# Attention scores and value products in quarters of TensorE's array, with blocks of 64 keys of two heads and other first loads

## The chip, the cores and the metric

The kernel runs on one core of a Trainium2 chip. The metric is the device time of one execution in microseconds (us); times of several executions are given by their median. The engines are named as in the profile: PE is TensorE (matmuls; its weight loads are PEld), DVE is VectorE, ACT is ScalarE, POOL is GpSimd, and SP is SyncE, which issues most of the DMAs.

## The reference

Eight batches of eight heads, 576 tokens, head dimension 64. Attention keeps, in each row of scores, only what lies within tau of the row's maximum; the result goes through a gated feed-forward block with a convolution of three taps along the tokens.

```python
scores = scale * np.matmul(q, k.transpose(0, 1, 3, 2))
thresh = np.max(scores, axis=-1, keepdims=True) - tau
scores = np.where(scores >= thresh, scores, -1000000000.0)
scores = scores - np.max(scores, axis=-1, keepdims=True)
attn = np.exp(scores)
attn = attn / (np.sum(attn, axis=-1, keepdims=True) + 1e-09)
attn_out = np.matmul(attn, v)
...
h = np.maximum(x @ w_in, 0.0)            # x: heads side by side, 512; h: 1024
conv_out += conv_w[k] * hp[:, k:k + S, :]  # k = 0, 1, 2
gate = 1.0 / (1.0 + np.exp(-conv_out))
return h * gate @ w_out
```

## The kernel before

**Tiling.** A batch's 576 queries are four tiles of 128 and one of 64. Two chunks split them: tiles 0 and 1 (256 queries) and tiles 2, 3 and 4 (320). For each chunk the kernel goes through four pairs of heads. A unit is one tile of queries of one pair. Everything is fp32; a product in fp32 stands in the trace as two matmul records, and the feed-forward splits its operands into high and low parts and takes three products.

**A unit** (`unit`, L526). For each of the two heads TensorE computes 128 x 576 scores (L549): the head dimension of 64 fills half of the array's rows, so the keys are laid out as two halves of 288 on the lower and upper 64 partitions, and two products run side by side, each on 64 rows and 128 columns of the array. Each half goes to a PSUM bank of its own (tile ps_s). VectorE takes the row's maximum (L558), ScalarE the exponential into em (L565), VectorE the mask with the sum (L568), and mostly GpSimd the normalization (L606). Tile 4 has 64 queries, so its unit takes both heads of a pair at once as 128 rows, in four products of 64 rows and 64 columns.

**Transposition.** em holds 1152 keys (both heads) in nine blocks of 128. Each must be turned so that keys lie on partitions (tile eT). Either TensorE transposes blocks into PSUM (ps_t, L665) in groups of four and ScalarE copies them (L660), or a unit is "crossed": it is split into 16-bit halves (L331, L333), written to memory and read back by transposing DMAs (`cross`, L621). The ninth block, and that of the small unit, hold keys of both heads or half a block, and are collected in a group of their own (`odd`, L694).

**Attend** (`attend`, L708). The product with v: one "mixed" step in quarters of the array for the block that holds keys of both heads (L720), then four steps per pair on 128 rows and 64 columns (L729). From the third chunk on two pairs are attended together (`JOINT = 2`), the first pair's four steps ahead of the second's. The sums stand in two PSUM buffers (pa, of the same two that ps_t uses), and ScalarE and VectorE take them out as high and low part (L736, L739).

**Feed-forward.** `mm1` (L758) and `mm2` (L809) use the whole array, and their pieces are strewn between the units of the next chunk.

**Order.** `Plan` records every operation with its reads, writes, cost and rank (place in the program less a lead from AHEAD) and then plays all engines through, so that each takes the ready operation of lowest rank; the order it finds is the program. SWITCH holds its cost of a change between forms of TensorE's work: "rows" (scores and mixed step), "cols" (the other attend steps), "turn" (transpositions), "full" (feed-forward).

**First loads.** `prep` (L488) loads k, q and v of a pair and scales k by an eighth. For the first pair k comes in two parts on ScalarE's queue, and ScalarE scales them; the first three pieces of the weights are issued on ScalarE's queue too (L380), the rest on SP's.

Of the kernel before, what the change touches and what calls it, by code (L numbers as in the profile page):

```python
# [22 lines left out]
AHEAD = {'mask': 0.543, 'norm': 2.382, 'parts': 0.64, 'gate': 1.279, 'evac': 0.244, 'low': 0.0, 's': 8.8, 's4': 8.664, 't': 3.225, 'a': 3.987, 'prep': 7.193, 'w': 2.513, 'load': 10.996}  # L23

LATENCY = {'pe': 159.52, 'act': 151.014, 'dve': 109.122, 'pool': 87.954, 'ring': 1611.881}

HOLD = {'pool': 133.132, 'dve': 108.982}

NORM = (('pool',), ('pool', 'pool', 'pool', 'act'))
# [5 lines left out]
MOE = (2, 3)  # L35
BACKLOG = {'pool': 6860.0, 'dve': 120.0, 'act': 9000000000.0}
WRATE = (1.767, 1.972)
ALT = 2.85
# [4 lines left out]
EARLY = 1  # L43
# [7 lines left out]
JOINT = 2  # L51

FAR = 3
VB = 4
EMS = 5
KEEPK = 1
# [5 lines left out]
CROSS = ((1, 1, 1, 1), (2, 1, 2, 1))  # L62
LATE = {'load': 663.0, 'copy': 114.0, 'rows': -19.0, 'turn': 737.0}

KEEP = {'rows': 3.449, 'cols': 2.129, 'turn': 2.26, 'full': 1.604}
# [187 lines left out]
def tile_tau_attention_gated_ffn(  # L253
    ctx: ExitStack,
    tc: tile.TileContext,
    qd: bass.AP,
    kp: bass.AP,
# [16 lines left out]
    NBLK = 2 * S // P  # L274
    TILES = [(t * P, min(P, S - t * P)) for t in range((S + P - 1) // P)]

# [32 lines left out]
    op("act", 450, lambda: nc.scalar.dma_start(tau_sb[:], tau.broadcast_to([P, 1])), w=[(tau_sb, 0)], ahead=205.0, late=2500)  # L309
# [3 lines left out]
    for x in fews:  # L313
        op("pool", 100, lambda x=x: nc.gpsimd.memset(x[:], LEAST * S), w=[(x, 0)], ahead=200.0)
        op(
            "dve", 150, lambda x=x: nc.vector.tensor_scalar(x[:, 1:4:2], x[:, 1:4:2], 0.0, tau_sb[:], op0=ALU.mult, op1=ALU.add),
            w=[(x, 0)], r=[(tau_sb, 0)], ahead=100.0
        )
# [7 lines left out]

    engines = {"dve": nc.vector, "pool": nc.gpsimd, "act": nc.scalar}
# [31 lines left out]
    def split(src, n, name, high, low, hr, lr, queue="sp"):  # L359
# [19 lines left out]
        def load():  # L379
            (nc.sync if queue == "sp" else nc.scalar).dma_start(flat().bitcast(I64), src)  # L380
# [17 lines left out]
        if queue == "sp":  # L398
            put(2 * n, load, issue=330, w=[hi, lo], ahead=w + AHEAD["load"])
        else:  # L400
            put(2 * n, load, issue=330, queue="act", w=[hi, lo], ahead=90)
# [66 lines left out]
    def load_weight(i):  # L468
        if i < W1N:
            src, dst, c, f = w_in, w1, i % NCB, i // NCB  # L470
        else:
# [4 lines left out]
            src[c * P:(c + 1) * P, f], WN, f"stage_{i}", h, l, *((x, (c, f.start)) for x in dst), "act" if i < 3 else "sp"  # L476
# [11 lines left out]
    def prep(i):  # L488
# [5 lines left out]
        k = whole[i - NP][0] if o and KEEPK else plan.buf(wk, "xk", XKB, [P, S + D], F32, f"k_{i}")  # L494
        q = plan.buf(wk, "q", QB, [P, 2, w], F32, f"q_{i}")
        a = AHEAD["prep"]

        if i:
            if not (o and KEEPK):
                put(S + D, lambda: nc.sync.dma_start(k[:], kp[b, p]), w=[(k, 0), (k, 1)], ahead=a + 2)  # L500
            put(w, lambda: nc.sync.dma_start(q[:], qd[b, p, :, :, o:o + w]), rows=2 * P, w=[(q, 0), (q, 1)], ahead=a + 2)
        else:
            for j, on in enumerate((slice(0, CH), slice(CH, S + D))):
                n = on.stop - on.start
                put(n, lambda on=on: nc.scalar.dma_start(k[:, on], kp[b, p, :, on]), queue="act", w=[(k, j)], ahead=210 - 10 * j)
                put(w, lambda j=j: nc.sync.dma_start(q[:, j], qd[b, p, :, j, o:o + w]), w=[(q, j)], ahead=210 - 10 * j)
        if not (o and KEEPK):
            cuts = [(S + D, lambda: k[:], [(k, 0), (k, 1)])] if i else [
                (on.stop - on.start, lambda on=on: k[:, on], [(k, j)]) for j, on in enumerate((slice(0, CH), slice(CH, S + D)))
# [440 lines left out]
```

## Time and profile before

| what | value |
|---|---|
| median of three runs | 882.54 us (882.46 to 882.92) |
| the profiled execution | 883.45 us, its span 881.7 us |
| granted TensorE clock, mean | 0.998 |
| instructions | 17007 |
| data moved by DMA | 141.53 MB, mean 161 GB/s |

The span runs from the first to the last instruction; what lies around it is 1.75 us here. A row of the groups by shape gives line, engine, operation, out<-in, partitions x elements and count, then busy us, mean ns of one, and the idle time of the engine before these with what ended it. For matmuls, "64*128" is the part of the array, rows by columns. A row of the stretches gives the stretch, its length, then the busy time of PE, PEld, DVE, ACT and POOL with counts, the granted clock, and the DMA share and GB/s. A timeline row gives start, length, engine, line and count of equal instructions merged.

### The profile page before, as it was taken

The page shows a single profiled execution, that of the slowest core. Times are in us where ns is not written, and L with a number is a line of the kernel's source. Part 1 is how long each engine was busy: PE and PEld are TensorE (multiplying, and loading weights), DVE is VectorE, ACT ScalarE, POOL GpSimd, SP SyncE. Part 2 cuts the span into 40 slices and gives each one's busy share as a digit, 9 for nine tenths or more (in the row PEclk, how much of TensorE's full clock was granted, in tenths as well). Part 3 has the DMA queues.
Part 4 walks back from the last instruction along what each step waited for, and adds up shares of the span by engine and source line. Part 5 has one row for each costly group of instructions (what it writes and reads, how often), then busy time and mean ns, then how long its engine had stood idle before and what let it go on. Part 6 is the DMA issues. An engine that isn't in the chain of part 4 may idle for free.

```text
span 881.7 us, 17007 instructions
## 1 busy us (share of the span) xinstructions
PE 851.9 (97%) x5678; PEld 617.5 (70%) x5678; DVE 724.6 (82%) x1905; ACT 670.9 (76%) x1327; POOL 422.2 (48%) x558
## 2 busy tenths in 40 slices
PE   2989999999999999999999999999999999999998
PEld 1445667767678677777778676776777777777796
DVE  3798999988979698987979789996979879996642
ACT  4889888888777687886868777886877868776642
POOL 1465645553546444563536434463544635564321
PEclk9999999999999999999999999999999999999999
DMA  7356136678766765858566675669566475556200
GB/s 257 110 158 191 57 99 169 170 224 213 163 162 161 187 188 148 193 155 235 158 162 139 199 202 161 164 166 237 161 173 146 141 210 158 151 165 159 67 25 37
DMA packets 211063, 141.53 MB, mean 161 GB/s; under 512 B 170144, under 2 KB 186784, under 8 KB 210976
## 3 DMA queue, kind: packets, MB, share of 16 engines
q1 hardware_dynamic: 210112, 138.54, 58.1%
q10 hardware_dynamic: 864, 1.90, 0.6%
q8 instruction: 46, 0.75, 0.3%
q14 instruction: 41, 0.34, 0.1%
HBM read 48.39 MB, written 50.72 MB: 112 GB/s over the span
## 4 chain that ended last, share of the span: by engine, by line
PE 91%; ACT 3%; DVE 3%; DMA 1%; issue 1%; SPq 0%; POOL 0%; ACTq 0%; DVEq 0%; POOLq 0%
PE ph L758 23%; PE po L809 23%; PE ps_s L549 19%; PE pa L729 14%; PE ps_t L665 9%; PE pa L720 2%; DVE few L558 1%; ACT em L565 1%; PE pw_stage L412 1%; DMA q<-in_qd_dram 1%; DVE em L568 1%; ACT eT L660 1%; DMA v<-in_vc_dram 0%; DVE stage_f L393 0%; ACT stage L387 0%
## 5 line engine op out<-in xcount | busy, mean ns | idle before, releaser
L606 POOL TENSOR_SCALAR em<-em,few 128x576 f32<-128x576 f32 x228 | 184.2, 815 | 185.4 <-DVE few L592 168.5
L558 DVE TENSOR_REDUCE few<-ps_s 128x1 f32<-128x576 f32 x288 | 209.3, 748 | 63.3 <-PE ps_s L549 62.7
L565 ACT ACTIVATE em<-ps_s,few 128x576 f32<-128x576 f32 x288 | 208.7, 740 | 56.4 <-DVE few L558 54.7
L568 DVE SCALAR_TENSOR_TENSOR em<-ps_s,few,em 128x576 f32<-128x576 f32 x288 | 226.9, 812 | 23.1 <-ACT em L565 14.2
L758 PE MATMUL ph<-x,w1h 128*128 128x322 f32 (+1 forms) x1024 | 231.8, 305 | 0.6 <-ACT hp L767 0.6
L338 POOL TENSOR_TENSOR gl<-t,gh 128x255 fp32r<-128x255 f32 (+9 forms) x192 | 122.0, 645 | 197.2 <-ACT gh L788 193.7
L549 PE MATMUL ps_s<-k,q 64*128 64x288 f32 (+1 forms) x1280 | 192.0, 439 | 17.6 <-ACT k L331 11.3
L758 PEld LDWEIGHTS ph<-x,w1h 128*128 128x128 f32 x1024 | 171.8, 190 | 16.1 <-issue 12.8
L549 PEld LDWEIGHTS ps_s<-k,q 64*128 64x128 f32 (+1 forms) x1280 | 94.1, 177 | 85.2 <-issue 44.4
L758 PE MATMUL ph<-x,w1l 128*128 128x322 f32 (+1 forms) x512 | 151.0, 295 | 0.0
L729 PE MATMUL pa<-eT,v 128*64 128x320 f32 (+1 forms) x1024 | 132.1, 409 | 0.0
L660 ACT ACTIVATE eT<-ps_t 64x64 f32<-64x64 f32 (+3 forms) x262 | 114.4, 452 | 16.3 <-PE ps_t L665 14.9
L809 PE MATMUL po<-w2h,gh 128*128 128x512 f32 x288 | 117.9, 410 | 0.0
L809 PE MATMUL po<-w2l,gh 128*128 128x512 f32 x288 | 112.7, 391 | 0.0
L809 PE MATMUL po<-w2h,gl 128*128 128x512 f32 x288 | 112.5, 391 | 0.0
L665 PE MATMUL ps_t<-ident,em 128*128 128x128 f32 x682 | 104.4, 281 | 7.6 <-ACT eT L660 3.5
L729 PEld LDWEIGHTS pa<-eT,v 128*64 128x64 f32 x1024 | 70.4, 137 | 58.8 <-issue 15.3
L665 PEld LDWEIGHTS ps_t<-ident,em 128*128 128x128 f32 x682 | 77.0, 141 | 45.6 <-issue 22.0
L758 PEld LDWEIGHTS ph<-x,w1l 128*128 128x128 f32 x512 | 96.5, 189 | 0.2
L331 ACT ACTIVATE parts<-em 128x1152 uint16<-128x1152 uint16 x70 | 81.4, 1163 | 19.0 <-POOL em L606 18.6
L773 DVE SCALAR_TENSOR_TENSOR t<-hp,cr 128x321 f32<-128x321 f32 (+1 forms) x128 | 81.7, 638 | 15.7 <-ACT hp L767 14.7
L333 POOL COPY parts<-em 128x1152 uint16<-128x1152 uint16 x70 | 82.7, 1182 | 15.1 <-DMA rows<-parts 6.9
(68 smaller groups left out, 924.1 us busy)
## 6 DMA issues: line engine op xcount, KB each, us to landing
rows<-parts SPq DMA_DIRECT2D x70, 576.0 KB, 3.1
v<-in_vc_dram SPq DMA_DIRECT2D x36, 288.0 KB, 4.3
q<-in_qd_dram SPq DMA_DIRECT2D x32, 320.0 KB, 3.5
k<-in_kp_dram SPq DMA_DIRECT2D x31, 320.0 KB, 4.1
out_dram<-ot SPq DMA_DIRECT2D x36, 256.0 KB, 3.1
q<-in_qd_dram SPq DMA_DIRECT2D x31, 256.0 KB, 3.4
stage<-in_w_out_dram SPq DMA_DIRECT2D x8, 512.0 KB, 3.5
stage<-in_w_in_dram SPq DMA_DIRECT2D x5, 512.0 KB, 4.2
```

The costliest lines, as they stand in the source:

```text
L333: engines[e].tensor_copy(dst, src)
L338: engines[e].tensor_tensor(dst, x, y, op=ALU.subtract)
L549: nc.tensor.matmul(ps[r * n:(r + 1) * n, c, :CH], lhsT=q[on, j, o:o + n], rhs=k[on, at:at + CH], start=True, stop=True)
L558: nc.vector.tensor_reduce(few[:rows, nm], ps[:rows, :, :CH], op=ALU.max, axis=mybir.AxisListType.XY, negate=True)
L565: nc.scalar.activation(view(), ps[:rows, :, :CH], AF.Exp, bias=few[:rows, nm])
L568: nc.vector.scalar_tensor_tensor(view(), ps[:rows, :, :CH], few[:rows, th], view(), op0=ALU.is_ge, op1=ALU.mult, accum_out=few[:rows, total])
L606: engines[e].tensor_scalar(sl, sl, LEAST, few[:rows, 10 + h:11 + h], op0=ALU.add, op1=ALU.mult)
L660: "act", act(w, True), lambda dst=dst, src=src: nc.scalar.activation(dst(), src(pt), AF.Copy),
L665: nc.tensor.transpose(out=pt[:, at:at + P], in_=em[:, int(b * P):int(b * P) + P], identity=ident[:])
L729: nc.tensor.matmul(pa[j * D:(j + 1) * D, :w], lhsT=vt[:, blk, :], rhs=eT[:, :w // D, blk, :], start=False, stop=(r == 3))
L758: nc.tensor.matmul(ph[:, :an], lhsT=w1[w][:, cb, fs], rhs=xs[cb][:, h, :an], start=(cb == 0 and i == 0), stop=(cb == NCB - 1 and i == 2))
L809: nc.tensor.matmul(po[:], lhsT=x[:, f, at:at + P], rhs=w[:, f, :], start=(f == 0 and i == 0), stop=(f == NFB - 1 and i == 2))
```

## The change

**Scores.** Every product is on 64 rows and 64 columns, four side by side: two halves of the keys by two groups of 64 queries. The keys of a head now stand as 288 and 288 around the border of two PSUM banks, so that the 576 scores of a row are contiguous. A small unit takes the last 64 queries of two pairs, both heads each (new input `qe`); k loses its 64 extra columns.

**Blocks.** em is written with runs of 64: a block of 128 is 64 adjacent keys of the first head and the same 64 of the second. So there is no odd block: each unit is nine blocks, transposed in groups of three, and every step of the attend is in quarters, nine steps for two pairs, with the pairs alternating. `JOINT = 0` attends two pairs together from the start. Units to be crossed are the first tile of each pair and the small units.

**First loads.** VectorE scales the first k; a copy on GpSimd (`gate`) from the second q half holds back all other early loads on SP's queue, and the weights come on that queue alone.

**The planner's tables** (AHEAD, LATENCY, KEEP, NORM and others) have new values; EARLY = 0 moves the second product of the first chunk one chunk later.

```diff
-JOINT = 2
-FAR = 3
+JOINT = 0
+BLOCKS = 3
+FAR = 4
-CROSS = ((1, 1, 1, 1), (2, 1, 2, 1))
+CROSS = ((1, 1, 1, 1), (1, 1, 1, 1), (1, 1))
...
+            def come():
+                nc.gpsimd.tensor_copy(gate[:], q[:, 1, :1])
+                nc.gpsimd.tensor_copy(second[:, :1], gate[:])
+            op("pool", 200, come, w=[(gate, 0), (second, 0), (second, 1)], r=[(q, 1)], ahead=205)
...
-                op("act", act(n), eighth, w=parts, ahead=a, other=[("pool", pool1(n)), ("dve", 65 + n * 0.53)] if i else [], port=True)
+                cost = {"act": act(n), "pool": pool1(n), "dve": 65 + n * 0.53}
+                home = "act" if i else "dve"
+                op(home, cost[home], eighth, w=parts, ahead=a, other=[(e, ns) for e, ns in cost.items() if i and e != home], port=True)
...
-                for r, j in enumerate(js):
-                    for c in range(2):
-                        on = slice(c * D, (c + 1) * D)
-                        at = j * CH + r * D
-                            ps[r * n:(r + 1) * n, c, :CH], lhsT=q[on, j, o:o + n], rhs=k[on, at:at + CH],
+                for c in range(2):
+                    on = slice(c * D, (c + 1) * D)
+                    for g, (q, k, _) in enumerate(sides):
+                            ps[g * D:(g + 1) * D, AT + c * CH:AT + (c + 1) * CH], lhsT=q(on, h), rhs=k[on, h * CH:(h + 1) * CH],
             def view(h=h):
-                return em[:rows, h * S:(h + 1) * S].rearrange("p (a b) -> p a b", a=2)
+                return em[:].rearrange("p (b j i) -> p j b i", j=2, i=D)[:, h]
...
+            def turns():
+                for i in range(n):
+                    block = em[:, (b0 + i) * P:(b0 + i + 1) * P]
+                    nc.tensor.transpose(out=pt[:, i * P:(i + 1) * P], in_=block, identity=ident[:])
...
+        for b0 in range(0, NBLK, BLOCKS):
+            group(b0, min(BLOCKS, NBLK - b0))
...
-        def mixed():
-            for (_, p, eT, vt, *_), pa in zip(of, pas):
-                for h in range(2):
-                    j, on = h ^ p % 2, slice(h * D, (h + 1) * D)
-                    nc.tensor.matmul(pa[j * D:(j + 1) * D, :w], lhsT=vt[on, 4, :], rhs=eT[on, :w // D, 4, :], start=True, stop=False)
-            for r in range(4):
-                        j, blk = h ^ p % 2, r + 5 * h
-                            pa[j * D:(j + 1) * D, :w], lhsT=vt[:, blk, :], rhs=eT[:, :w // D, blk, :], start=False, stop=(r == 3)
+        for step in range(NBLK):
+            def mm(step=step):
+                for (_, p, eT, vt, *_), pa in zip(of, pas):
+                    for h in range(2):
+                        j, on = h ^ p % 2, slice(h * D, (h + 1) * D)
+                            pa[j * D:(j + 1) * D, :w], lhsT=vt[on, step, :], rhs=eT[on, :w // D, step, :],
+                            start=(step == 0), stop=(step == NBLK - 1)
+            op("pe", w * 4 / 2.4 + 6, mm, w=[(pa, 0) for pa in pas], r=read, ahead=a, kind="rows")
```

Three places in the order of the two programs (rows hold line, operation, out<-in and size; the numbers in names count buffers).

TensorE before, at the first joint attend of the seventh batch, pairs 48 and 49 (ps_s: scores, pa: sums of the attend, po: feed-forward):

```order
L549 MATMUL ps_s_126_0_7401<-k_51_6687,q_51_7273 128x288 x2
L549 MATMUL ps_s_126_1_7409<-k_51_6687,q_51_7273 128x288 x2
L720 MATMUL pa_48_7416<-eT_48_7211,v_48_6956 64x256 x2
L720 MATMUL pa_49_7419<-eT_49_7325,v_49_6961 64x256 x2
L729 MATMUL pa_48_7416<-eT_48_7211,v_48_6956 64x256 x8
L729 MATMUL pa_49_7419<-eT_49_7325,v_49_6961 64x256 x8
L549 MATMUL ps_s_127_0_7460<-k_51_6687,q_51_7273 128x288 x2
```

TensorE after, the last two of the nine steps of the same attend:

```order
L720 MATMUL pa_48_8168<-eT_48_7997,v_48_7722 64x256 x2
L720 MATMUL pa_49_8171<-eT_49_8045,v_49_7736 64x256 x2
L569 MATMUL ps_s_115_0_8221<-k_51_7336,q_51_7915 64x288 x4
L720 MATMUL pa_48_8168<-eT_48_7997,v_48_7722 64x256 x2
L720 MATMUL pa_49_8171<-eT_49_8045,v_49_7736 64x256 x2
L569 MATMUL ps_s_115_1_8234<-k_51_7336,q_51_7915 64x288 x4
L801 MATMUL po_22_8105<-w2h_766,gh_1146 128x512
```

Scores, mixed step and the 128*64 steps were three forms; now all is one, scores are put between steps, and both pairs' sums end together.

TensorE before, transpositions of unit 139 among pieces of the feed-forward (ph):

```order
L665 MATMUL ps_t_139_0_8242<-ident_100,em_139_8176 128x128 x4
L665 MATMUL ps_t_139_4_8248<-ident_100,em_139_8176 128x128 x4
L549 MATMUL ps_s_141_0_8256<-k_56_6860,q_56_8044 128x288 x2
L758 MATMUL ph_12_2_8232<-x_50_7711,w1h_187 128x256
L758 MATMUL ph_12_2_8232<-x_50_7711,w1l_207 128x256
```

TensorE after, transpositions of unit 122:

```order
L684 MATMUL ps_t_122_0_8974<-ident_99,em_122_8786 128x128 x3
L801 MATMUL po_26_8960<-w2h_766,gh_1146 128x512
L801 MATMUL po_26_8960<-w2h_766,gl_1181 128x512
L801 MATMUL po_26_8960<-w2l_813,gh_1146 128x512
L684 MATMUL ps_t_122_3_8988<-ident_99,em_122_8786 128x128 x3
L684 MATMUL ps_t_122_6_8992<-ident_99,em_122_8786 128x128 x3
```

A unit's nine blocks were two groups of four and one collected with others; now they are three groups of three, with feed-forward work between them.

ScalarE's first rows before (k, stage: first weights; em: exponential):

```order
L505 DMA k_79<-in_kp_dram 128x288
L309 DMA tau_sb<-in_tau_dram 128x1
L325 ACT_TABLE_LOAD
L325 ACTIVATE warm<-warm 128x1
L505 DMA k_79<-in_kp_dram 128x352
L380 DMA stage_113<-in_w_in_dram 128x512
L380 DMA stage_118<-in_w_in_dram 128x512
L380 DMA stage_125<-in_w_in_dram 128x512
L331 ACTIVATE k_79<-k_79 128x288
```

SP's first rows after:

```order
L515 DMA q_81<-in_qd_dram 128x256 x2
L510 DMA k_119<-in_kp_dram 128x576
L511 DMA q_130<-in_qd_dram 128x2x256
L386 DMA stage_133<-in_w_in_dram 128x512
L545 DMA v_136<-in_vc_dram 128x576
L545 DMA v_141<-in_vc_dram 128x576
L510 DMA k_145<-in_kp_dram 128x576
L386 DMA stage_152<-in_w_in_dram 128x512
L386 DMA stage_161<-in_w_in_dram 128x512
```

The three weight loads left ScalarE's queue, where they stood ahead of the first scaling of k; on SP's queue they stand behind the other k, q and two v.

More of the change, by code (lines that the diff above doesn't have):

```diff
@@ L475, in load_weight @@
         split(
[L476 removed]
+            src[c * P:(c + 1) * P, f], WN, f"stage_{i}", h, l, *((x, (c, f.start)) for x in dst), "first" if i < 3 else "load"
         )
@@ L574, in unit @@
                 "pe", 490, mm, w=[(ps, 0)],
-                r=[(x, j) for x in (k, q) for j in js], ahead=a, kind="rows"
+                r=[x for _, k, r in sides for x in ((k, h), *r(h))], ahead=a, kind="rows"
             )
@@ L615, in unit, with crossed, cross @@
         return em
-    def crossed(i, t):
-        c, p = pairs[i]
-        return chunks[c].b > 0 and t in [x for x in order(i) if TILES[x][1] == P][:CROSS[c % 2][p]]
-    def cross(u, em, eT, off):
+    def crossed(c, p, n):
+        if chunks[c].b == 0:
+            return False
+        return n < CROSS[c % 2][p] if n is not None else CROSS[2][p // 2]
+    def cross(u, em, dsts):
         parts = plan.buf(wk, "parts", PTB, [P, 2, 2 * S], U16, f"parts_{u}")
@@ L840, in tile_tau_attention_gated_ffn, with units_of @@
     xs = {}
-    def order(i):
-        c, p = pairs[i]
-        return chunks[c].tiles[::-1] if p % 2 else chunks[c].tiles
     pairs = [(c, p) for c in range(len(chunks)) for p in range(NP)]
-    units = [(i, t) for i in range(len(pairs)) for t in order(i)]
-    whole, vts = {}, {}
+    def units_of(c):
+        tiles = [t for t in chunks[c].tiles if TILES[t][1] == P]
+        for p in range(0, NP, 2):
+            for i in (c * NP + p, c * NP + p + 1):
+                for n, t in enumerate(tiles):
+                    yield i, t, n
+            if len(tiles) < len(chunks[c].tiles):
+                yield c * NP + p, chunks[c].tiles[-1], None
+    units = [x for c in range(len(chunks)) for x in units_of(c)]
+    counts = [len(list(units_of(c))) for c in range(len(chunks))]
+    whole, made, vts, lasts, eTs = {}, {}, {}, {}, {}
     prep(0)
@@ new lines, in tile_tau_attention_gated_ffn @@
+            em = unit(now, sides, n is None)
+            if crossed(c, p, n):
+                cross(now, em, dsts)
+            else:
+                transposes(now, em, dsts)
+            if n == 0:
+                prep(i + 1)
+            ends = now + 1 == len(units) or units[now + 1][0] // 2 != i // 2
+            alone = c < JOINT and w == 2 * P
+            if ends or alone and units[now + 1][0] != i:
+                waiting = []
+                for x in [i // 2 * 2, i // 2 * 2 + 1] if not alone else [i]:
+                    xp = x % NP
+                    y = plan.buf(wk, f"x{c % 2}", NP, [P, 2, XW[c % 2]], F32R, f"x_{x}")
+                    xs.setdefault(c, []).append(y)
+                    off = o - a0
+                    if off:
+                        z, end = xs[c - 1][xp], chunks[c - 1].cols[1]
+                        op(
+                            "pool", 110, lambda y=y, z=z, off=off, end=end: nc.gpsimd.tensor_copy(y[:, :, :off], z[:, :, end - off:end]),
+                            w=[(y, 2)], r=[(z, 0), (z, 1)]
+                        )
+                    waiting.append((x, xp, eTs[x], vts[x], y, off))
+                attend(waiting, w, [x for x in plan.wrote if any(x[0] is y[2] for y in waiting)])
@@ L889, in tile_tau_attention_gated_ffn @@
+            if now + 1 == len(units) or pairs[units[now + 1][0]][0] != c:
                 seq = ffn(c)
```

254 lines of the change are left out of this document (114 added, 140 removed).

## The prediction

> **What bounds the kernel now.** I read the page's busy shares and its chain of waits first, then the stretches, then the groups by shape.
>
> ```profile
> PE 851.9 (97%) x5678; PEld 617.5 (70%) x5678; DVE 724.6 (82%) x1905; ACT 670.9 (76%) x1327; POOL 422.2 (48%) x558
> PE 91%; ACT 3%; DVE 3%; DMA 1%; issue 1%; SPq 0%; POOL 0%; ACTq 0%; DVEq 0%; POOLq 0%
> 0.00:10.00 10.00, 0.69 (x4) 0.50 (x4) 0.62 (x4) 2.67 (x5) 0.98 (x14) 1.00 0.77 245
> 10.00:20.00 10.00, 4.38 (x16) 1.57 (x12) 6.14 (x14) 4.84 (x10) 1.00 (x1) 1.00 0.74 281
> 60.00:80.00 20.00, 16.63 (x99) 9.30 (x97) 17.17 (x45) 18.91 (x35) 11.54 (x13) 0.91 0.56 171
> sum 700.00, PE 698.59 PEld 510.58 DVE 601.03 ACT 546.58 POOL 344.71; mean PE 99.80 PEld 72.94 DVE 85.86 ACT 78.08 POOL 49.24
> 860.00:882.00 22.00, 17.98 (x83) 14.81 (x82) 5.37 (x10) 6.01 (x12) 3.97 (x4) 1.00 0.10 37
> ```
>
> TensorE makes up 91% of the chain and is busy for 851.9 of 881.7 us. The sum row covers the seven stretches of 100 us from 120 to 820: there TensorE idles 1.4 us of 700, while VectorE has 99 us to spare, ScalarE 153. So for four fifths of the span the time is what TensorE's instructions cost. Of its 30 us of idle time nearly all lies in the first 120 us (the first 20 us alone hold 15) and about 4 at the end.
>
> What TensorE pays is read from start to start, since ends are modelled:
>
> ```profile
> 408.45 0.66 PE L665 MATMUL ps_t<-ident,em 128*128 128x128 f32 x4
> 408.87 0.36 PE L758 MATMUL ph<-x,w1h 128*128 128x256 f32 x1
> ...
> 410.81 0.76 PE L549 MATMUL ps_s<-k,q 64*128 64x288 f32 x4
> 411.50 0.38 PE L758 MATMUL ph<-x,w1h 128*128 128x256 f32 x1
> ...
> 407.28 1.24 PE L549 MATMUL ps_s<-k,q 64*128 64x288 f32 x8
> ...
> 526.61 0.77 PE L720 MATMUL pa<-eT,v 64*64 64x320 f32 x8
> 527.31 4.53 PE L729 MATMUL pa<-eT,v 128*64 128x320 f32 x32
> 531.76 1.24 PE L549 MATMUL ps_s<-k,q 64*128 64x288 f32 x8
> ...
> 567.68 1.20 PE L549 MATMUL ps_s<-k,q 64*64 64x288 f32 x16
> 568.70 0.61 PE L720 MATMUL pa<-eT,v 64*64 64x256 f32 x8
> 569.24 3.67 PE L729 MATMUL pa<-eT,v 128*64 128x256 f32 x32
> 572.85 1.24 PE L549 MATMUL ps_s<-k,q 64*128 64x288 f32 x8
> ...
> 771.98 1.20 PE L549 MATMUL ps_s<-k,q 64*64 64x288 f32 x16
> 773.11 0.42 PE L758 MATMUL ph<-x,w1h 128*128 128x322 f32 x1
> ```
>
> One head of scores in the wide form (64*128) takes 0.69 us to the next kind's start (410.81 to 411.50), two take 1.17 (407.28 to 408.45). So a head streams for 0.485 and **leaving that form costs 0.20**. Two small units in quarters (64*64) take 1.13 up to the feed-forward (771.98 to 773.11): the same two times 0.485, and **0.16 for leaving**. Up to the mixed step of the attend, quarters too, they take 1.02: 0.05 for leaving, almost nothing. So four quarters do in 0.485 us what two halves do, and quarters followed by quarters pay no change.
>
> **The change part by part.**
>
> *Scores.* 256 heads in the wide form become quarters, and 32 stay so: each streams 0.485 as before. By the order of both kernels TensorE leaves wide scores 155 times now and quarters 9 times on its own account; afterwards it leaves quarters 136 times, because scores and attends stand next to each other without a change of form. 155 x 0.20 + 9 x 0.16 = 32.4 us become 136 x 0.16 = 21.8: **-10.6**. If quarters cost 0.20 to leave as well, it is -5.2.
>
> *Attends.* A joint one takes 0.70 + 4.45 us at 320 columns (526.61 to 531.76) and 0.54 + 3.61 at 256; TensorE has 14 of each. The four single pairs at either width in the first batch take half the columns' part and the whole mixed step, 2.9 and 2.4 us. Sum 72.1 + 58.1 + 11.6 + 9.6 = 151.4 us. Afterwards there are 16 + 16 joint ones of nine quarter steps. A step at 320 columns is a quarter pass scaled by width, 0.485 x 320/288 = 0.539, at 256 it is 0.431: 16 x 9 x (0.539 + 0.431) = 139.7 us, leaving already counted above: **-11.7**. From the other side, if nine sustained steps cost what a step of the 128*64 run does (4.45/8 = 0.556 and 3.61/8 = 0.451), it is 145 us, -6.4.
>
> *Transpositions.* 682 become 666, and groups of four blocks become groups of three.
>
> ```profile
> L665 PE MATMUL ps_t<-ident,em 128*128 128x128 f32 x682 | 104.4, 281 | 7.6 <-ACT eT L660 3.5 <-POOL em L606 2.8 <-issue 1.2
> L660 ACT ACTIVATE eT<-ps_t 64x64 f32<-64x64 f32 (+3 forms) x262 | 114.4, 452 | 16.3 <-PE ps_t L665 14.9
> L660 ACT ACTIVATE eT<-ps_t 128x512 f32<-128x512 f32 x148 | 86.0, 601 | 9.6 <-PE ps_t L665 9.3
> L660 ACT ACTIVATE eT<-ps_t 128x256 f32<-128x256 f32 x8 | 3.3, 414 | 0.0
> L816 ACT ACTIVATE ot<-po 128x512 f32<-128x512 f32 x36 | 21.5, 597 | 23.4 <-PE po L809 23.0
> ```
>
> Four take 0.42 us start to start (408.45 to 408.87), so 16 fewer are -1.7. Smaller groups are fitted into the feed-forward more often: by the order the step from feed-forward to transpositions is made 95 times instead of 66. No row shown has this step by itself: it costs nothing at one end and the 0.2 of leaving scores at the other. I charge the middle, 29 x 0.1 = +2.9 (0 to 5.8). For ScalarE a copy of 384 columns lies between the 414 and 601 ns rows, at 508; 216 of these and 12 of half the width come to 114 us, what the 262 copies take now. No change.
>
> These parts give -21.1. As quarters were never many in a row so far, I take **-20**, with a range from -7.5 (all poorer ends) to -24 (all better ones).
>
> *Small units.* 32 single-head-pair units become 16 of two, which takes 16 sets of three tiny VectorE instructions away (L562, L589 and L592, two of them shown).
>
> ```profile
> L592 DVE RECIPROCAL few<-few 128x1 f32<-128x1 f32 x32 | 4.9, 157 | 0.3
> L589 DVE TENSOR_REDUCE few<-few 128x1 f32<-128x2 f32 x32 | 4.6, 146 | 0.1
> L568 DVE SCALAR_TENSOR_TENSOR em<-ps_s,few,em 128x576 f32<-128x576 f32 x288 | 226.9, 812 | 23.1 <-ACT em L565 14.2
> L606 POOL TENSOR_SCALAR em<-em,few 128x576 f32<-128x576 f32 x228 | 184.2, 815 | 185.4 <-DVE few L592 168.5
> ```
>
> At about 0.15 us each that is 7 us of VectorE, which lies beside TensorE and so counts nothing.
>
> *Layout of em.* Exponential, mask and normalization now write runs of 64 with gaps of 64. On ScalarE the copy into eT already writes runs of 64 and takes 601 ns where a contiguous one of the same size takes 597, so I cost it at nothing there. For VectorE's mask (812 ns) and GpSimd's normalization (815) no row shows it: nothing at one end, half as long again at the other. GpSimd is half idle. VectorE covers its part with its 99 us of spare time: seven batches hold 252 masks, so 0.39 us more for each would use it up. I take nothing, nearest to the eT row.
>
> *First loads.*
>
> ```profile
> 0.74 0.88 SPq L506 DMA_DIRECT2D q<-in_qd_dram  x2
> 3.67 5.10 ACTq L380 DMA_DIRECT2D stage<-in_w_in_dram  x3
> 8.82 1.07 ACT L331 ACTIVATE k<-k 128x288 f32<-128x288 f32 x2 [5.65 <-DMA q<-in_qd_dram]
> 12.12 0.49 ACT L331 ACTIVATE k<-k 128x352 f32<-128x352 f32 x1
> 12.66 1.33 PE L549 MATMUL ps_s<-k,q 64*128 64x288 f32 x4 [2.02 <-ACT k L331]
> 21.23 1.12 PE L665 MATMUL ps_t<-ident,em 128*128 128x128 f32 x4 [2.76 <-POOL em L606]
> q<-in_qd_dram SPq DMA_DIRECT2D x2, 128.0 KB, 3.3
> k<-in_kp_dram ACTq DMA_DIRECT2D x1, 144.0 KB, 2.9
> ```
>
> The first k half lands 2.9 us after its issue, near 4 us, and the q halves near 5. But ScalarE issues three weight loads until 8.77 and only then scales k; the second half waits behind an exponential until 12.12. Afterwards VectorE, idle then, scales both; the weights go to SP's queue, and they, the other k, q and v wait for a copy that GpSimd makes when q has come. I expect the first head near 5 us instead of 9.3, the second behind it instead of 12.66, and the first transpositions near 14 instead of 21.2. Against that, 3 MB follow only from 5 us on, some 12 us at the 245 to 281 GB/s of the first rows, where the weights are awaited from 12.5 us. I take **-5**, from 0 to -8.
>
> *What is lost.* In the first batch (an eighth of the work) TensorE isn't the bound alone: ScalarE is busy for 18.91 of 20 us from 60 to 80, so an eighth of the -20 turns into idle time: **+2.5**. New waits: both pairs of an attend now end at the same moment, where the first pair used to be ready some 2 us earlier, so both transposition buffers come free late.
>
> ```profile
> L739 DVE TENSOR_TENSOR x<-pa,x 128x320 fp32r<-128x320 f32 x32 | 15.6, 486 | 13.8 <-ACT x L736 13.8
> L736 ACT ACTIVATE x<-pa 128x320 fp32r<-128x320 f32 x32 | 14.0, 438 | 16.0 <-PE pa L729 15.3
> ```
>
> Two copies and a subtraction behind them, 1.4 us, must pass, and by the order at least 1.4 us of other TensorE work stands behind each of the 32, mostly 2 us or more. I charge 0.1 each, **+3**.
>
> Sum on the profiled execution: span 881.7 - 20 - 5 + 2.5 + 3 = 862.2, with the 1.75 us around the span 864.0. This execution took 883.45, 0.9 above the median, so **863**.
>
> **The rivals.**
>
> *Savings taken back by waits (16 in 100).* If ScalarE or VectorE stand in a long instruction (0.8 us) when an attend ends, TensorE waits for its transposition buffers: 32 x 0.5 = 16 us, about 876. For it: both engines are 78 and 86% busy. Against: the work placed behind each attend. The Trainium skill, page "TensorEngine Tiling (Array Packing)", section "PSUM Bottleneck", warns of just this, that tiling quickens TensorE and not the emptying of PSUM; the 1.4 us of idle time from 120 to 820 shows none of it with today's tiling.
>
> *VectorE becomes the bound (5 in 100), slower.* If gaps of 64 make a mask 0.39 us longer, VectorE has no slack from 120 to 820; from there on each 0.1 us adds 25 us. At 0.5 us more the time is about 907. Only the eT row, of another engine, speaks against it.
>
> *Quarters do not run side by side (2 in 100), slower.* The new order issues two products on the same 64 rows one after the other, where small units changed rows each time. Were these two serial, each head would take 0.485 more, 256 x 0.485 = 124 us: near 987. Against: the mixed step uses the same rows for two pairs and takes 0.54 at 256.
>
> *Each record has a price (2 in 100).* There are 2,032 matmul records more. Sixteen took 1.02 us, of which 0.97 is streaming, so at most 3 ns each: 6 us, 869. The Trainium skill, same page, section "Instruction Overhead", gives about 60 cycles to a matmul and advises against splitting what is small; at 25 ns that would be 51 us, an estimate from that page, near 914 and slower than before, to which I give another 2 in 100. The sixteen records speak against it.
>
> *More than forecast (7 in 100).* All of -24 and -8 and no new waits would be 853; half of that surplus, 858, still lies in the forecast.
>
> **How the numbers follow.** The forecast, 856 to 870, has 62 in 100, and 4 are left for about no change, where waits take back all. 853 to 878 holds the forecast and most of the neighbouring rivals; the 9 on the slower side, the 4 near no change and some 7 of the others lie outside. A measurement here tells 0.2% (1.8 us) from no change. Faster 0.87 (62 forecast, 16 waits, 7 more, 2 records at 3 ns), same 0.04, slower 0.09 (5 VectorE, 2 serial quarters, 2 records at the page's price).
>
> **What would show it.** Right: wide and 128*64 forms gone, two heads of quarters 1.13 us start to start, nine steps 4.85 us at 320 columns, the first head near 5 us, idle time of TensorE under 5 us from 120 to 800. Wrong: a mask over 1.1 us, waits of transpositions on the pa buffers, a first transposition later than 18 us, or quarters that leave for 0.2 us and more.

## The result and the profile after

| | before | after |
|---|---|---|
| median | 882.73 us (882.46 to 883.63, 4 runs) | 858.67 us (857.31 to 860.76, 4 runs) |
| ratio | 1 | 0.9728, 95% interval 0.9704 to 0.9752 |
| profiled execution | 883.45 us, span 881.7, clock 0.998 | 857.31 us, span 855.2, clock 1.000 |

The changed kernel is 24.1 us faster by the medians, 26.5 by the spans of the two profiled executions. The forecast was 863, with a range of 853 to 878.

The busy shares and the chain of waits of the changed kernel, from its page:

```profile
PE 830.0 (97%) x7710; PEld 609.3 (71%) x7710; DVE 719.6 (84%) x1869; ACT 656.7 (77%) x1300; POOL 410.9 (48%) x549
PE 86%; ACT 7%; DVE 4%; DMA 1%; issue 1%; POOL 0%; SPq 0%; DVEq 0%; ACTq 0%
```

TensorE is busy for 21.9 us less (851.9 before) with 2,032 more records. Its idle time went from 29.8 us (881.7 - 851.9) to 25.2. So 21.9 of the 26.5 us came out of TensorE's own work and 4.6 out of its idle time; in the chain ScalarE went from 3 to 7%.

Where the idle time lies, from the stretches (length, busy time of each engine with its instructions, granted clock, DMA share, GB/s); the first sum is over six stretches of 20 us, the second over seven of 100 us from 120 to 820:

```profile
0.00:10.00 10.00, 3.69 (x29) 1.58 (x32) 4.53 (x15) 3.85 (x6) 1.36 (x16) 1.00 0.49 139
60.00:80.00 20.00, 16.02 (x128) 8.21 (x120) 18.29 (x51) 19.89 (x38) 11.38 (x14) 1.00 0.69 214
sum 120.00, PE 100.82 PEld 62.65 DVE 105.74 ACT 105.38 POOL 62.21; mean PE 16.80 PEld 10.44 DVE 17.62 ACT 17.56 POOL 10.37
sum 700.00, PE 697.62 PEld 518.38 DVE 599.21 ACT 537.90 POOL 340.79; mean PE 99.66 PEld 74.05 DVE 85.60 ACT 76.84 POOL 48.68
```

In the first 120 us TensorE idles 19.2 us. The same six stretches of the kernel before are this one row:

```profile
sum 120.00, PE 95.70 PEld 57.68 DVE 96.36 ACT 97.28 POOL 59.91; mean PE 15.95 PEld 9.61 DVE 16.06 ACT 16.21 POOL 9.99
```

That is 24.3 us before. From 120 to 820 it idles 2.4 us after and 1.4 before. VectorE has 101 us to spare there, as it had 99.

The start, from TensorE's timeline (start, duration, line, out<-in, part of the array, count, and the idle time before with what ended it):

```profile
4.08 2.20 PE L569 MATMUL ps_s<-k,q 64*64 64x288 f32 x16 [4.08 <-DVE k L341]
8.50 2.20 PE L569 MATMUL ps_s<-k,q 64*64 64x288 f32 x16 [2.23 <-DVE em L591]
12.25 0.90 PE L684 MATMUL ps_t<-ident,em 128*128 128x128 f32 x3 [1.55 <-POOL em L629]
```

Both first heads run at 4.08 us (the first at 9.3 before) and the first transposition at 12.25 (21.23 before).

The prices in the steady part, from the same timeline:

```profile
406.50 1.20 PE L569 MATMUL ps_s<-k,q 64*64 64x288 f32 x16
407.63 0.39 PE L750 MATMUL ph<-x,w1h 128*128 128x256 f32 x1
...
408.53 5.08 PE L720 MATMUL pa<-eT,v 64*64 64x320 f32 x72
413.43 1.15 PE L569 MATMUL ps_s<-k,q 64*64 64x288 f32 x16
414.51 0.39 PE L750 MATMUL ph<-x,w1h 128*128 128x256 f32 x1
```

Two heads of quarters up to the feed-forward take 1.13 us (406.50 to 407.63): the prediction's 0.97 of streaming and 0.16 for leaving. The nine steps at 320 columns and two heads behind them take 5.98 (408.53 to 414.51). That is the sum of the prediction's 4.85 and the same 1.13, which leaves nothing between attend and scores.

The instructions whose layout or size changed, from the groups (operation, shapes, count, busy us, mean ns, idle time before):

```profile
L591 DVE SCALAR_TENSOR_TENSOR em<-ps_s,few,em 128x576 f32<-128x576 f32 x288 | 224.8, 812 | 12.9 <-ACT em L588 5.6
L588 ACT ACTIVATE em<-ps_s,few 128x576 f32<-128x576 f32 x288 | 207.6, 745 | 56.9 <-DVE few L581 56.1 <-DVE few L615 0.3
L694 ACT ACTIVATE eT<-ps_t 128x384 f32<-128x384 f32 x216 | 102.3, 505 | 19.7 <-PE ps_t L684 18.8 <-ACT t L772 0.7
```

The mask costs 812 ns as before, with runs of 64 and gaps. The copy of three blocks takes 505 ns, estimated at 508.

What TensorE waits for from 120 to 820, after (us in total, times, longest):

```profile
PE ps_s L569 <- DVE em L591: 1.2, 2, 0.7
PE ps_s L569 <- issue: 0.8, 1, 0.8
```

No transposition waits for a pa buffer there. Two of the three waits, 1.2 us, are scores that wait for a bank which VectorE's mask has still to read; for the third the profile shows no cause.

### The profile page after: what moved, and what is told of

Read it like the earlier page. It is cut to its first block, busy times and chain, and to the rows that moved or that the text cites. A ratio compares the mean times of both kernels' runs of the same rounds, so it can differ in the third digit from the quotient of the medians.

```text
span 855.2 us, 20928 instructions
## 1 busy us (share of the span) xinstructions
PE 830.0 (97%) x7710; PEld 609.3 (71%) x7710; DVE 719.6 (84%) x1869; ACT 656.7 (77%) x1300; POOL 410.9 (48%) x549
## 4 chain that ended last, share of the span: by engine, by line
PE 86%; ACT 7%; DVE 4%; DMA 1%; issue 1%; POOL 0%; SPq 0%; DVEq 0%; ACTq 0%
PE ph L750 24%; PE po L801 23%; PE ps_s L569 17%; PE pa L720 15%; PE ps_t L684 8%; ACT em L588 2%; ACT eT L694 1%; DVE em L591 1%; DVE few L581 1%; DMA stage<-in_w_in_dram 1%; ACT stage_f L389 1%; PE pw_stage L415 0%; ACT stage L393 0%; ACT em L627 0%; DMA q<-in_qd_dram 0%
## 5 line engine op out<-in xcount | busy, mean ns | idle before, releaser
L629 POOL TENSOR_SCALAR em<-em,few 128x576 f32<-128x576 f32 x217 | 172.8, 804 | 199.1 <-DVE few L615 175.6
L750 PE MATMUL ph<-x,w1h 128*128 128x322 f32 (+1 forms) x1024 | 237.3, 308 | 0.0
L569 PE MATMUL ps_s<-k,q 64*64 64x288 f32 x2048 | 164.4, 423 | 10.9 <-DVE em L591 5.5
L720 PE MATMUL pa<-eT,v 64*64 64x256 f32 (+1 forms) x2304 | 153.8, 404 | 0.0
L720 PEld LDWEIGHTS pa<-eT,v 64*64 64x64 f32 x2304 | 91.4, 133 | 49.2 <-issue 1.5
L694 ACT ACTIVATE eT<-ps_t 128x384 f32<-128x384 f32 x216 | 102.3, 505 | 19.7 <-PE ps_t L684 18.8
L569 PEld LDWEIGHTS ps_s<-k,q 64*64 64x64 f32 x2048 | 67.0, 134 | 68.0 <-issue 24.7
L765 DVE SCALAR_TENSOR_TENSOR t<-hp,cr 128x321 f32<-128x321 f32 (+1 forms) x128 | 78.5, 614 | 22.2 <-ACT hp L759 21.3
L772 ACT ACTIVATE t<-t,cm 128x321 f32<-128x321 f32 (+1 forms) x128 | 68.6, 538 | 27.3 <-DVE t L765 21.1
```

Source lines behind the costliest of these rows:

```text
L569: nc.tensor.matmul(ps[g * D:(g + 1) * D, AT + c * CH:AT + (c + 1) * CH], lhsT=q(on, h), rhs=k[on, h * CH:(h + 1) * CH], start=True, stop=True)
L629: engines[e].tensor_scalar(sl, sl, LEAST, few[:, 10 + h:11 + h], op0=ALU.add, op1=ALU.mult)
L694: "act", act(n * P, True), lambda: nc.scalar.activation(eT[:, g:g + 2, b0:b0 + n, :], source(), AF.Copy),
L720: nc.tensor.matmul(pa[j * D:(j + 1) * D, :w], lhsT=vt[on, step, :], rhs=eT[on, :w // D, step, :], start=(step == 0), stop=(step == NBLK - 1))
L750: nc.tensor.matmul(ph[:, :an], lhsT=w1[w][:, cb, fs], rhs=xs[cb][:, h, :an], start=(cb == 0 and i == 0), stop=(cb == NCB - 1 and i == 2))
```

## The experiments

Each kernel ran beside the kernel before on the same chip. Since the medians of the latter differ a little (881.56 to 882.96), kernels are compared by their ratios to it, times 882.5 us.

**The changed kernel again (after_again).**

> The changed kernel as it is, timed on the same chip as the next three, so that they can be set against it: 857 to 861 us as in its first four executions.

859.19 us (858.27 to 859.70), ratio 0.9733 (0.9719 to 0.9747). Two measurements of the same kernel lie 0.4 us apart.

**Scores as wide products again (wide).** The order of all engines stays as in the changed kernel, product for product; the scores of the 256 large heads go back to two products on 64 rows and 128 columns.

```diff
+                    if not small:
+                        nc.tensor.matmul(
+                            ps[:, AT + c * CH:AT + (c + 1) * CH], lhsT=sides[2](on, h), rhs=sides[0][1][on, h * CH:(h + 1) * CH],
+                            start=True, stop=True
+                        )
+                        continue
...
```

> The changed kernel, with the scores of the 256 heads that share one tile of queries as two products on 64 rows and 128 columns again in place of four on quarters; every engine's order is the changed kernel's, row by row. Theory (the gain is in the changes of form that TensorE no longer pays): wide scores are left 148 times at 0.20 us, 41 of these towards an attend step and 61 towards the feed-forward, and quarters 60 times at 0.16, 39.2 us in place of 136 x 0.16 = 21.8: +17 us, 875 to 878. Rival (the gain is in the blocks, the layout and the new order, and quarters are only another way to write the same): within 2 us of the changed kernel, 857 to 861. Second rival (only the price of leaving scores for other engines' work counts, 0.04 more each for 107): +4 us, 863.

871.77 us (871.19 to 873.48), ratio 0.9880 (0.9861 to 0.9898): 13.0 us slower than the changed kernel. Wide scores in the midst of an attend, from TensorE's timeline of this kernel:

```profile
334.61 3.68 PE L726 MATMUL pa<-eT,v 64*64 64x256 f32 x64
338.22 1.24 PE L569 MATMUL ps_s<-k,q 64*128 64x288 f32 x8
339.39 0.66 PE L726 MATMUL pa<-eT,v 64*64 64x256 f32 x8
```

Its busy shares, from its page:

```profile
PE 847.1 (97%) x6686; PEld 624.3 (72%) x6686; DVE 720.2 (83%) x1869; ACT 657.9 (76%) x1300; POOL 408.9 (47%) x549
```

Those of after_again:

```profile
PE 830.9 (97%) x7710; PEld 609.8 (71%) x7710; DVE 719.3 (84%) x1869; ACT 657.0 (77%) x1300; POOL 410.7 (48%) x549
```

Two wide heads take 1.17 us up to the next step (338.22 to 339.39), where quarters stream the same scores in 0.97; leaving the attend for them costs on top (its eight steps take 3.61 us up to the scores, 334.61 to 338.22, and eight steps at 0.431 are 3.45). TensorE is busy for 16.2 us more than in after_again, about the 17 expected, with 1,024 records fewer: it is the changes of form that cost, not the records. Of the 16.2 us, 13 to 14 reach the end; idle time falls from 25.3 to 23.0.

**The first loads alone, in the kernel before (before_first).** VectorE scales the first k, the weights go to SP's queue, the GpSimd copy holds the rest back; the tables stay as before but for the places of tau and of these weights.

```diff
...
-            (nc.sync if queue == "sp" else nc.scalar).dma_start(flat().bitcast(I64), src)
+            nc.sync.dma_start(flat().bitcast(I64), src)
...
+            def come():
+                nc.gpsimd.tensor_copy(gate[:], q[:, 1, :1])
+                nc.gpsimd.tensor_copy(second[:, :1], gate[:])
...
+                home = "act" if i else "dve"
...
```

> The kernel before with the changed kernel's first loads alone: VectorE scales the first k, weights on SP's queue, other early loads held back until q has come. Theory: first scores near 4 to 5 us, total -5, 876 to 879. Rival (it only pays together with the new order): no change, 881 to 884.

877.61 us (877.46 to 878.50), ratio 0.9944 (0.9932 to 0.9957): 4.9 us faster than the kernel before. Its first matmul, from the timeline:

```profile
3.98 2.29 PE L562 MATMUL ps_s<-k,q 64*128 64x288 f32 x8 [3.98 <-DVE k L336]
```

Its first 120 us, from the stretches:

```profile
sum 120.00, PE 103.10 PEld 62.90 DVE 106.71 ACT 102.93 POOL 62.19; mean PE 17.18 PEld 10.48 DVE 17.78 ACT 17.16 POOL 10.36
```

The first loads bring the 5 us of the prediction. TensorE's idle time there falls from 24.3 to 16.9.

**The first loads undone in the changed kernel, order planned anew (first_undone).**

```diff
...
-            nc.sync.dma_start(flat().bitcast(I64), src)
+            (nc.scalar if lead == "first" else nc.sync).dma_start(flat().bitcast(I64), src)
...
+            put(2 * n, load, issue=330, queue="act", w=[hi, lo], ahead=90)
...
-                home = "act" if i else "dve"
+                home = "act"
```

> The changed kernel with the first loads as they were: weights 0 to 2 on ScalarE's queue, ScalarE scales the first k, nothing waits for q. Theory (first loads bring some 5 us by an earlier start, and the rest of the kernel keeps it): first scores near 9.3 us, total +5, 862 to 866. Rival (the first batch is bound by ScalarE and VectorE, so an earlier first score is waited away later): first scores near 9.3 all the same, total within 2 us, 857 to 861. Second rival (they bring more than 5, since all of the first transpositions come 9 us earlier): +8 or more, above 866.

872.36 us (871.25 to 873.81), ratio 0.9884 (0.9869 to 0.9900): 13.3 us slower than the changed kernel. That is what the second rival expected, but the run doesn't part it from the theory: with other costs the planner made the order of the whole first batch anew, and TensorE's idle time there is 29.3 us. The granted clock was lower too, 0.991 to 0.994 in its four executions against 0.996 to 0.998 in after_again's, and TensorE is busy for 834.3 us with the same products (830.9 there).

**The same, with the order kept (first_same).** The three loads are written out early on ScalarE's queue and ScalarE scales the first k, while every other instruction stays in its place on its engine.

```diff
...
+        early = [x for x in emit if getattr(x[0], "early", False)]
+        for n, (fn, e, new) in enumerate(emit):
+            if n == 16:
+                for f, _, _ in early:
+                    f(e)
...
-                nc.gpsimd.tensor_copy(second[:, :1], gate[:])
...
-                    copy(e, x(), x(), 0.125)
+                    copy(e if i else "act", x(), x(), 0.125)
```

> The changed kernel with its planned order kept on every engine, but with the first loads as the kernel before has them: three weight loads on ScalarE's queue ahead of the scaling of the first k, that scaling on ScalarE, and no copy on GpSimd that holds the other k, q and v back. Theory (the first loads are worth the 5 us that they brought when put alone into the kernel before; the rest of the 13 us of first_undone came from the order that the planner made anew): 864 us, 5 above the changed kernel, with the first matmul some 4 us later and TensorE's idle time of the first 120 us at 24 instead of 19. Rival (with quarters the first loads themselves are worth 13): 872 us.

862.57 us (861.34 to 863.73), ratio 0.9777 (0.9763 to 0.9792): 3.9 us slower than the changed kernel. TensorE's first matmul, from the timeline:

```profile
9.13 2.20 PE L580 MATMUL ps_s<-k,q 64*64 64x288 f32 x16 [9.13 <-ACT k L347]
```

Its first 120 us, from the stretches:

```profile
sum 120.00, PE 96.01 PEld 59.42 DVE 101.34 ACT 101.96 POOL 58.73; mean PE 16.00 PEld 9.90 DVE 16.89 ACT 16.99 POOL 9.79
```

The first matmul is 5 us later and 24.0 us are idle, close to the theory. So the first loads are worth 4 to 5 us with quarters as without. The other 9 us of first_undone came with an order planned anew: against this run 5.7 us more of idle time (36.0 and 30.3 in all) and 3.4 us more of busy time, under the lower clock. This run is also the change without its first loads: 19.7 us under the kernel before.

**The hold alone taken away (nogate_same).** The order is kept; the GpSimd copy that holds back the second k, and with it all that stands behind on SP's queue, is left out.

```diff
-                nc.gpsimd.tensor_copy(second[:, :1], gate[:])
```

> The changed kernel with its order kept, but without the GpSimd copy that holds the second k, and behind it on SP's queue the other q, v and the weights, back until the first q has come. Theory (the gain of the first loads lies in where the first k is scaled and in the weights leaving ScalarE's queue; the hold is nearly worthless): within 1.5 us of the changed kernel, 858 to 860, first matmul within 1 us of 4.1. Rival (the first q and k come late when 3 MB run beside them; the hold carries the gain): 3 to 5 us more, first matmul at 6 us or later.

858.10 us (857.15 to 859.66), ratio 0.9719 (0.9706 to 0.9732); the first matmul is at 3.93 us, although SP issues the second k at 1.68 us instead of 5.14. The hold is worth nothing that shows: the 4 to 5 us come from where the first k is scaled and from what stands ahead of it. No run parts these two.

**Two quarters at a time in the first batch (apart_c0).** In the attends of the first batch at one width the pairs follow one another within the attend, instead of alternating.

```diff
+        todo = [(x, pa, s) for x, pa in zip(of, pas) for s in range(NBLK)]
...
-                for (_, p, eT, vt, *_), pa in zip(of, pas):
+                both = todo[2 * step:2 * step + 2] if of[0][0] < NP else [(x, pa, step) for x, pa in zip(of, pas)]
+                for (_, p, eT, vt, *_), pa, s in both:
...
```

> The changed kernel in the same order, but in the first batch's attends at one width the two pairs come one after the other within each attend instead of alternating, so that two quarters run at a time instead of four: some 8 us more of TensorE's time between 30 and 75 us, the same sums. Theory of the prediction (in the first batch TensorE is not the bound, what it saves or loses there turns into idle time): at most 3 us more than the changed kernel, TensorE's busy time up 8 and its idle time of the first 120 us down by 5 or more. Rival (the first batch counts like the rest, which would explain why the 2.5 us charged as hidden did not appear): 8 us more, near 867.

863.56 us (862.04 to 864.67), ratio 0.9785 (0.9769 to 0.9800): 4.6 us slower, between the two. TensorE is busy for 837.3 us, 6.4 more than in after_again, and idle for 24.2 instead of 25.3. Neither expectation held as written: most of what TensorE does in the first batch counts, and by these two executions about a fifth of this was hidden.

**Two quarters at a time in all attends (apart).** The same edit without its condition, a single run.

> The changed kernel with the two pairs one after the other in all attends, so that two quarters run at a time instead of four; same products, same sums. If four quarters of an attend really run side by side in the changed kernel, each of its 32 joint attends takes twice as long: 139 us more, near 997. If the array takes quarters one after the other anyway, or is limited by something that four share, it stays near 859. The share in between is how far the four overlap.

963.01 us, 80.6 above the median before and 104 above the changed kernel. How many of the attend's records run in one microsecond (the stretches of that line alone; the count stands behind the busy time and holds every record that runs at some time in the stretch), in apart early in an attend and in its middle, at 256 columns:

```profile
395.00:396.00 1.00, 1.00 (x12) 1.00 0.00 0
398.00:399.00 1.00, 1.00 (x19) 1.00 0.09 25
```

The same of the changed kernel, at 256 columns too:

```profile
450.00:451.00 1.00, 1.00 (x24) 1.00 0.00 0
```

12 against 24: the four quarters run fully side by side when pairs alternate. The cost was 104 us and not 139. The trace shows why it is less: more than two run at once in the middle of an attend, where the second pair's products begin beside the last of the first (19), and at its end, where the next scores begin, as apart's timeline shows:

```profile
400.97 0.45 PE L569 MATMUL ps_s<-k,qe 64*64 64x288 f32 x1
401.17 0.38 PE L722 MATMUL pa<-eT,v 64*64 64x256 f32 x2
401.26 0.40 PE L569 MATMUL ps_s<-k,qe 64*64 64x288 f32 x1
401.39 0.38 PE L722 MATMUL pa<-eT,v 64*64 64x256 f32 x2
```

In the program all 72 records of this attend stand ahead of these scores. The scores on the two free quarters start before the attend's last products on the two others.

**ScalarE relieved in the first batch (kpool, kpool_same, kpool_late).** The scaling of k goes from ScalarE to GpSimd: in kpool for pairs 1 to 9 with the order planned anew, in kpool_same for the same five instructions that stood on ScalarE, with the order kept, in kpool_late for three of these.

```diff
-                home = "act" if i else "dve"
+                home = "pool" if 0 < i < 10 else "act" if i else "dve"
```

> The changed kernel with the scaling of k of pairs 1 to 9 on GpSimd instead of ScalarE, about 6 us less for ScalarE in the first batch, and an order that the planner made anew. If ScalarE bounds the first batch from 60 to 80 us (it is busy for 19.9 of 20 there), the time falls by 2 to 6 us, to 853 to 857. If the first batch waits on something else (loads, VectorE's masks), it stays within 1 us of 859, or rises where GpSimd is late with a k.

```diff
-                    copy(e, x(), x(), 0.125)
+                    copy("pool" if 0 < i < 10 and e == "act" else e, x(), x(), 0.125)
```

> The changed kernel with its order kept, but five scalings of k in the first batch (some 0.75 us each) stand on GpSimd at the same place of the program instead of on ScalarE; nothing else moves, unlike kpool, where the planner made the whole order anew. If kpool lost its 8 us by the new order and ScalarE does bound the first batch, this is 1 to 4 us faster than the changed kernel: 855 to 858. If a k that comes late from GpSimd holds scores up, it is slower by 1 to 5 us, and TensorE's waits on GpSimd's k show it. If ScalarE is not what the first batch waits for: within 1 us of 859.

> As kpool_same, but only for the pairs from the fourth on (three scalings), so that the first two, which stand near the start where GpSimd's normalizations are awaited, stay on ScalarE. If ScalarE bounds the first batch: 1 to 2 us faster than the changed kernel, 856.5 to 858; and faster than kpool_same if that one loses by its first two. If not: within 1 us of 859.

kpool took 867.39 us (865.09 to 868.46), ratio 0.9829 (0.9812 to 0.9846), 8.5 slower; kpool_same 858.10 (857.51 to 859.10), 0.9720 (0.9707 to 0.9733); kpool_late 857.97 (857.88 to 859.06), 0.9720 (0.9707 to 0.9733). From 20 to 40 us in kpool, from the stretches:

```profile
20.00:40.00 20.00, 15.62 (x160) 8.97 (x153) 17.99 (x45) 16.73 (x34) 14.44 (x13) 1.00 0.35 109
```

The same in kpool_same:

```profile
20.00:40.00 20.00, 17.18 (x180) 10.63 (x172) 18.59 (x51) 17.16 (x37) 15.04 (x17) 1.00 0.46 146
```

In both ScalarE, the fourth of the busy times, has the relief (19.14 in the changed kernel). TensorE gains nothing by it: 15.62 us busy in kpool and 17.18 in kpool_same, against 17.58. Five scalings stand on GpSimd in both, and only kpool loses by it: its loss too came with an order planned anew. The five scalings lay before 40 us, so the stretch from 60 to 80 was not touched.

**ScalarE relieved from 60 to 80 us (relief60).** Two normalizations and two scalings go to GpSimd, in the same place of the order.

```diff
-                    copy(e, x(), x(), 0.125)
+                    copy("pool" if 9 < i < 12 and e == "act" else e, x(), x(), 0.125)
...
+                e = "pool" if u in (11, 13) and e == "act" else e
```

> The changed kernel with its order kept, but four instructions of ScalarE between 67 and 87 us (two normalizations of 0.91 and 0.94 us, two scalings of k of 0.75 and 0.88 us) stand on GpSimd at the same place of the program: ScalarE, which is busy for 19.9 of 20 us from 60 to 80, gets 2.6 us of these 20 back. kpool_same relieved it only before 40 us. Theory (ScalarE holds TensorE up in this stretch): TensorE's busy time from 60 to 80 rises from 16.0 by 1 us or more and the time falls by 1 to 3 us, to 855 to 857.5. Rival (several engines and the round trip from scores to transpositions hold it up together): within 1 us of 858, TensorE's busy time from 60 to 80 within 0.5 of 16.0. A GpSimd that comes late would show as waits of transpositions on its normalization, and 1 us or more of loss.

857.39 us (855.71 to 858.32), ratio 0.9717 (0.9698 to 0.9736). The stretch in this kernel:

```profile
60.00:80.00 20.00, 16.62 (x136) 9.15 (x129) 18.94 (x52) 19.48 (x38) 16.37 (x18) 1.00 0.69 221
```

GpSimd has taken the work (16.37 against 11.38). ScalarE fills most of the gap with what stood behind, and TensorE gains 0.6 us. That lies between the theory (1 us or more) and the rival (at most 0.5), and the time of 857.4 us lies in the range of both. So relief of ScalarE alone frees little here; what else holds the first batch up was not taken apart. kpool_same, kpool_late and relief60 can't be told from the changed kernel in time.

## Why the prediction was right

**Changes of form and attends, forecast -21.1, taken as -20.** TensorE's busy time fell by 21.9. The prices were right to the hundredth where the timeline shows them: 0.16 for leaving quarters, 4.85 us for nine steps, nothing between attend and scores. after_again is the fairer profile to set beside the kernel before, since each of the two has one stretch of 3.4 us at half clock in the first batch and the changed kernel's first profile has none; there the fall is 21.0. That this total is not right by large errors that cancel can be read from the two traces. Take each record's time from its start to the next one's start, less idle time, and add it up by kind:

| kind | before, us | after_again, us | difference | forecast |
|---|---|---|---|---|
| scores | 179.0 | 167.2 | -11.8 | -13.7 |
| attends | 152.5 | 143.5 | -9.0 | -8.7 |
| transpositions and feed-forward | 503.9 | 505.1 | +1.2 | +1.2 |
| splitting the weights | 16.5 | 15.0 | -1.5 | 0 |

(The forecast counted the 19 times that the new attends are left, 3.0 us, with the scores; in the table they stand with the attends.) wide tests the price of the forms by itself: with wide scores in the same order TensorE pays 16.2 us more, expected at 17, and the same addition puts 10.9 of it on the scores and 5.2 on the attends beside them. That the plain sum was cut from 21.1 to 20 for quarters that run long was needless; this is 1.0 to 1.9 us of the 4.3 by which the forecast was too high.

**First loads, -5.** before_first gives -4.9, first_same +3.9 for their removal. The start was right in its steps (first head near 5, measured 4.08; first transposition near 14, measured 12.25). The prediction left open how much the hold matters; nogate_same shows no effect of it.

**What is lost, +2.5 hidden and +3 new waits.** These are the terms that were mis-sized. Without the first loads on either side (the kernel before and first_same) idle time goes from 29.8 to 30.3 us, +0.5. With them on both sides (before_first, 875.8 - 853.2 = 22.6 us idle, and the changed kernel, 25.2) it is +2.6. So 0.5 to 2.6 us came of the 5.5. New waits in the steady part are small: idle time from 120 to 820 rose by 1.0 us, and none of the waits there stands on the pa buffers. The order put other work behind each attend, as the prediction had counted, and the 0.1 us charged for each of 32 was not there. The other term took all that TensorE saves in the first batch to turn into idle time, with ScalarE's 18.91 of 20 us as the reason. apart_c0 hides only a fifth of its 6.4 us, and relief60 gives ScalarE time back without much gain. How much of the first batch is hidden is not settled to better than 2 us: of the 16.2 us of wide, some 2 should lie in the first batch, and about as much was hidden.

**The sum.** From the forecast of 863: 1.0 to 1.9 us for TensorE's work that fell by more, and some 3 for the losses that came smaller, make 858 to 859; 858.67 was measured. The spans of the two profiles of the changed kernel lie 7.0 and 6.0 us under the forecast span of 862.2, 5 of them in idle time. Executions of one kernel spread over 3.5 us, so the rest can't be told apart more finely.

**The rivals.** Savings taken back by waits: of its 16 us, 1.0 came. The Trainium skill's warning, in "TensorEngine Tiling (Array Packing)", section "PSUM Bottleneck", that emptying PSUM may become the limit, doesn't bite here: from 120 to 820 ScalarE and VectorE keep 162 and 101 us free, and nothing waits for a pa buffer. VectorE as the bound: the mask stayed at 812 ns. Quarters in series: apart shows what that would look like, 12 records in a microsecond instead of 24, and a time of 963. A price for each record: 2,032 more records stand beside a fall of 21.9 us, and wide has 1,024 fewer and is slower. By the rule of the Trainium skill, same page, section "Instruction Overhead", some 60 cycles for each matmul, 914 was an estimate; no such addition shows for quarters that follow one another.

## What to carry to other kernels

Where one engine is busy for 97%, count what it pays between instructions as well as in them: here two forms of the same product streamed at the same speed, and the gain lay in letting neighbours have one form. Price each change of form from start to start of neighbouring instructions, count the changes in the new order, and here the sum held to 1 us in 22. In a program whose order a planner makes, undo a part with the order kept: the two experiments that let it plan anew lost some 9 us each with the new order, more than the parts that they were to measure.

## What the runs showed of the hardware that was not expected

Products on free quarters of the array start ahead of earlier products that wait for busy quarters: in apart the next scores start at 400.97 us, attend products that stand ahead of them in the program at 401.17 and 401.39. So an order that isn't perfectly alternating can cost less than counting quarters would say (104 us instead of 139, by a single run).

Scaling k by a constant takes GpSimd twice as long as its normalization of as many elements, by the groups of kpool_same, though the spans of this engine are rough. Why was not tried:

```profile
L341 POOL TENSOR_SCALAR k<-k 128x576 f32<-128x576 f32 x5 | 8.3, 1652 | 2.9 <-DMA k<-in_kp_dram 2.9
L629 POOL TENSOR_SCALAR em<-em,few 128x576 f32<-128x576 f32 x217 | 172.7, 803 | 193.0 <-DVE few L615 164.0 <-PE ps_s L569 18.2 <-DMA rows<-parts 7.2
```

The same kernel on the same inputs spreads over 3.5 us with the granted clock: of the four runs of the changed kernel the two at 1.000 have spans of 855.2 and 855.5 us, the two at 0.996 spans of 857.6 and 858.7. In after_again the lower clock stands in one stretch of the first batch, and within it in single microseconds:

```profile
40.00:60.00 20.00, 17.02 (x156) 9.61 (x155) 17.71 (x55) 17.45 (x34) 9.18 (x11) 0.91 0.45 147
46.00:47.00 1.00, 0.00 (x0) 0.00 (x0) 1.00 (x3) 1.00 (x4) 1.00 (x2) 1.00 0.00 0
50.00:51.00 1.00, 1.00 (x12) 1.00 (x13) 1.00 (x4) 0.40 (x2) 0.57 (x1) 0.50 0.73 197
53.00:54.00 1.00, 1.00 (x11) 0.37 (x13) 0.91 (x3) 0.83 (x2) 0.16 (x1) 1.00 0.51 68
```

So 0.91 is not a clock that is a little lower: it was half for some 3.4 us, from 49.4 to 52.8, and full beside it. TensorE had paused shortly before. In first_undone, where TensorE idles most (36.0 us), the trace has the half clock for 13.6 us of the first 120. In the changed kernel's own profile the stretch from 40 to 60 has 1.00 throughout, after nearly the same pause (TensorE busy for 2.34 us from 44 to 48, 2.35 in after_again). What decides whether a pause lowers the clock was not tried.
